# Last weights' decoding every 7 products in two expert tiles, and attention's row weighings ranked among its operations

## The chip, the cores and the metric

The kernel runs on one core of one Trainium2 chip. The metric is the device time of one execution in microseconds; the median of several runs counts. In what follows TensorE (PE) multiplies matrices, VectorE (DVE), ScalarE (ACT) and GpSimd (POOL) work on elements, and SyncE (SP) issues most of the transfers.

## What is computed

Three stages follow one another, all in float32:

```python
# 1. attention: 2 batches x 8 heads, 576 positions, 64 per head, rotary embedding
attn = softmax(rotate(q) @ rotate(k).T / 8);  x = (attn @ v)      # 1152 tokens x 512
# 2. experts: each token goes to one of 8 experts
logits = x @ w_gate + modality_bias[modality_id];  e = argmax(logits);  p = softmax(logits)[e]
y = p * (relu(x @ w1[e]) @ w2[e])                                 # 512 -> 1024 -> 512
# 3. last feed-forward
h = y @ w_in;  g = h * tanh(log1p(exp(h)));  out = g @ w_out      # 512 -> 2048 -> 512
```

## The kernel before

**Precision.** Every float32 product is done as three products of a high and a low half: high x high, high x low, low x high. ScalarE makes a high half by a copy, VectorE or GpSimd the low half by a subtraction. So one product group of an expert tile's first layer has 4 x 3 = 12 TensorE products, one of the second layer 8 x 3 = 24.

**Attention and its plan.** The operations of attention are given to a planner (class Plan) with an engine, a cost, a rank (the smaller, the earlier) and what they depend on. The planner simulates the engines' queues and so fixes each engine's order: when an engine is free, it takes the ready operation of lowest rank among the first 40 of its list, or else the one that can start earliest. Ranks near the end of attention lie between 140 and 176: the last maxima of the scores at about 151 and 154, the low halves of the transposed probabilities up to 158, the normalisations at 155.5, 156.1, 166.2 and 175.7. Into this plan the start of the experts is woven: once half of the tokens are routed, the first expert tile's 304 rows are loaded (xrow), weighed by their gate value on VectorE (x_gate, L1301, three row tiles of 128, 128 and 48 rows), transposed on TensorE (x_tr, L1312, into banks of the scores) and split into halves (x_hi, x_lo). These operations have rank 900, behind all of attention. Beside them GpSimd starts on the low halves of the expert weights (L611).

**Expert tiles.** Four tiles of 304 rows follow, two for each half of the tokens; here they are called tiles 1 to 4. A tile has 8 groups of 12 products (hidden layer, L705; after each a relu on ScalarE, L728, and the low half of it on VectorE, L730), then 4 groups of 24 products (output, L705), and four transposed row groups of the next tile (L669, L676) after the second of them. Expert weights come in chunks of 512 KB. PSUM has seven buffers for the products.

**Decoding of the last weights.** The weights of stage 3 come as 16 chunks of 1 MB of 64-bit numbers, through two buffers (wr, L1382), and VectorE makes float32 chunks (wc) of them with three operations: L1398, L1403, L1408. During the expert tiles each operation handles half a chunk (512 columns) and goes through a PSUM tile (rt); a chunk is then six counts. In the last stage an operation handles 1024 columns and counts two. The next load into a buffer is issued by SyncE two counts after the chunk in it is done. While tiles are computed, `drive` takes up a count whenever a running counter of TensorE steps is a multiple of `every`:

```python
if y[0] != "pe":
    continue
nq_[0] += 1
if nq_[0] % every == 0:
    decode(1, limit)
```

The value of `every` is `P['dec'][0]`, 12, for tiles 1 and 2 (no decoding in the last two groups of tile 2), `P['dec'][1]` for tile 3 and `P['dec'][2]` for tile 4, where the limit is 72 counts, twelve chunks. Before tile 1's products reach `drive`, the routing of the second half of the tokens has drawn some of them ahead.

**Last stage.** It runs over two groups of tokens (640 and 512) and, in each, over 16 chunks of the hidden width. For each chunk TensorE makes h (L1578, 12 products for each half of the tokens, three PSUM buffers), ScalarE three steps towards tanh (L1593 to L1597), VectorE a reciprocal (L1604) and a multiplication that also frees the buffer of h (L1605), ScalarE and GpSimd the halves of g (L1616, L1622), and TensorE adds the chunk's share to the output (o, L1639). Its order is written out by times in units of half a chunk. Decoding is put into it in two ways, in the first group of tokens:

```python
if 3 <= q < FC2:
    at2(m + 0.6, decode, 2)
if q < FC2:
    for z in range(3):
        at2(m - 4.05 + 0.6 * z, lambda n=6 * q + 2 * z + 2: decode(n - nd[0]))
```

Of the kernel before, what the change touches and what calls it, by code (L numbers as in the profile page):

```python
# [35 lines left out]
FC2 = F2 // 128  # L36

Q = {'r0': 2.45, 'rd': 2.0, 'tanh': 1.06, 'rec': 1.1, 'hi': 2.2, 'lo': 2.38, 'o': 3.86}
P = {'sd': (4,), 'dl': (28, 44), 'qd': (2, 3), 'alt': (0.1, 4), 'd0': 82, 'vl': 24, 'w3': 3, 'rq': (0.2, 2.3, 0.55, 0.25), 'dec': (12, 9, 8), 'rl': 3, 'ah': 0, 'eps': 0.05, 'slack': 0.1}
K = {'ld': -22.67, 'prep': (-24.92, -22.38, -23.33, -27.14, -20.49, -7.62), 'sc': (-8.42, -3.18, 1.68, 1.67, 2.84, 10.44, 1.99, 8.05, 9.75), 'max': (-2.26, -5.46, -1.21, -1.85, 5.06, 8.41, 4.71, 11.42, 13.72), 'exp': (-3.19, 1.66, 6.32, 3.7, 13.26, 11.14, 14.6, -2.87, 25.74), 'tr': (0.69, 2.1, 2.56, 2.68, 5.53, 7.5, 8.45, 9.85, 10.88, 11.85, 15.56, 16.66, 16.92, 19.98), 'hi': (-3.91, -0.31, 2.51, 3.62, 4.25, 4.9, 5.01, 5.32, 7.26, 9.77, 13.56, 14.12, 14.6, 15.66), 'lo': (0.77, 1.83, 5.61, 6.34, 6.67, 7.32, 10.02, 10.73, 12.18, 13.92, 13.94, 14.62, 17.33, 18.02), 'pv': (7.08, 7.84, 10.5, 10.69, 14.13, 14.25, 14.32, 15.96, 18.04, 20.31, 21.03, 22.86, 23.97, 25.61), 'evac': (14.53, 9.65, 6.27, 25.13), 'rec': (-4.7, -0.45, 4.11, 12.71), 'fmm': (4.53, -3.79, 16.24, 17.22), 'norm': (15.5, 16.11, 26.18, 35.69)}  # L40

QT = [(0, 128), (128, 128), (256, 64), (320, 128), (448, 128)]
# [31 lines left out]
class Plan:  # L74
# [39 lines left out]
    def pick(self, e):  # L114
        best, lines = None, set()
        for o in self.todo[e][:40]:
# [8 lines left out]
            if best is None or t < best[0] - 1e-9:  # L125
                best = (t, o)
            if t <= self.free[e] + P["eps"]:
                break
# [40 lines left out]
    def run(self):  # L169
# [3 lines left out]
        while any(self.todo.values()):  # L173
            best = None
            for e in self.todo:
                c = self.pick(e)
                c = c and (c[0], 1, c[1])
                for o in self.alt[e][:4]:
# [4 lines left out]
                    t = max(t, self.free[e])  # L183
                    if (c is None or t + o[4] - P["alt"][0] <= c[0]) and t + o[4] + P["alt"][1] < end:
                        c = (t, 1, o)
                for st in self.streams:
# [3 lines left out]
                    if st["gate"] and not st["gate"](t):  # L190
                        continue
                    if c is None or t + (st["next"][1] - P["slack"] if e in st["low"] else 0.0) <= c[0]:
                        c = (t, 0, st)
# [19 lines left out]
def moe_kernel(ctx: ExitStack, tc: tile.TileContext, aps, out):  # L213
# [17 lines left out]
    def heads(x):  # L231

        return x[..., 0:XC].rearrange("p j (h e) -> p j h e", h=H)
# [325 lines left out]
    xrow, wraw, whl = {}, {}, {}  # L559
# [15 lines left out]
    def load_rows(k):  # L575
        r = regs[k]
        pool = mp if k != "x" else wpool[-1]
        xrow[k] = t = pool.tile([128, 3, RW], F32, tag="xrow", name=f"xrow{k}")
        for i, (r0, rn) in enumerate(TCH):
            ld = nc.sync.dma_start(out=t[:rn, i], in_=scratch[ds(r["c"] + r0, rn), :])  # L580
            if k != "x":
                after_scatters(ld, k[0])
# [18 lines left out]
    def split_chunk(k, i):  # L601
# [5 lines left out]
        lo = pool.tile([128, 1024], F32R, tag="wlo", name=f"wlo{k}_{i}", bufs=n)  # L607
        dve = k == (0, 0) and i in P["sd"]
        yield ("dve", 1.14, False) if dve else ("pool", 2.3, False)
# [71 lines left out]
    def moe_tile(k, feed, bank):  # L681
# [28 lines left out]
        for f in range(FC1):  # L710
# [7 lines left out]
            )  # L718
            if f == P["rl"] and nxt in regs and nxt not in feed.rows:
                feed.rows.add(nxt)  # L720
# [13 lines left out]
        for d in range(KC):  # L734
            i = 4 + d
            ends = k == (0, 1)
            if ends and d >= P["qd"][0]:
                yield "quiet"
# [79 lines left out]


    def attention(actx, hook):  # L820
        a_c = actx.enter_context(tc.tile_pool(name="a_const", bufs=1))
        p2 = actx.enter_context(tc.tile_pool(name="a_p2", bufs=2))
# [404 lines left out]
        op("ids", "act", 0.1, 30.0, setup_ids)  # L1227
        op("bias", "pool", 2.5, 60.0, setup_bias, deps=[("ids",)])
        hook(plan, bank, ltile)
        plan.run()  # L1230

# [12 lines left out]
    def route(b):  # L1244
        yield from routing(b, lambda: cur["rbank"]())

    def tile_rows(b):
        for i in range(2):
            regs[b, i] = tile_regs(tbl[b][:, i])

    def until_pe(gen):
        for y in gen:
            if y[0] in ("pe", "mark"):
                return
            yield y

    def hook(plan, bank, ltile):

        r0 = route(0)
        cur["rbank"] = lambda: bank("counts")  # L1260

        def until_mark():
            for y in r0:
                if y[0] == "mark":
                    return
                yield y

        def mark(name):
            return lambda t: plan.done.update({name: ("dve", t)})

        def start():
            plan.add(until_pe(r0), plan.now, end=mark("rt"), gate=cur["spare"])

        def rest():
            next(r0)
            plan.add(until_mark(), plan.now + 1.0, end=mark("rt_row"))

        def scatter():
            plan.add(cur["scatters"], plan.now, low=("pool",), end=mark("rt_sc"))

        def table():
            plan.add(r0, plan.now, end=mark("rt_end"))

        def weights():
            tile_rows(0)
            load_rows(K0)
            feed.rows.add(K0)
            plan.done["xrow"] = ("sp", plan.now + 7.8)
            plan.add(until_pe(gen0), plan.now + 3.9, low=LOW)

        K0, n0, xg = (0, 0), B * H - 1, []

        def x_gate(i):
            x, rn = xrow[K0], TCH[i][1]
            if not xg:
                gated.add(K0)
                t = mp.tile([128, FC1, T], F32R, tag="hl", name=f"xg{K0}").bitcast(F32)
                xg.append(t.rearrange("p a t -> p (a t)")[:, 0:3 * DM].rearrange(
                    "p (i d) -> p i d", i=3
                ))  # L1300
            nc.vector.tensor_scalar(  # L1301
                out=xg[0][:rn, i].rearrange("p (h e) -> p h e", h=H),
                in0=heads(x)[:rn, i, :, 0:D], scalar1=x[:rn, i, XC + 1:XC + 2], scalar2=None,
                op0=ALU.mult,
            )

        def x_bank(c):
            return ltile[3 + c // 2][:, c % 2]

        def x_tr(c, i):  # L1310
            r0, rn = TCH[i]
            nc.tensor.transpose(  # L1312
                out=x_bank(c)[:, r0:r0 + rn], in_=xg[0][:rn, i, c * 128:(c + 1) * 128],
                identity=ident[:rn, :rn],
            )

        def x_hi(c):
            if K0 not in xsplit:
                xsplit[K0] = tuple(
                    mp.tile([128, KC, T], F32R, tag=t, name=f"{t}{K0}") for t in ("xh", "xl")  # L1320
                )
            nc.scalar.activation(out=xsplit[K0][0][:, c], in_=x_bank(c)[:, :T], func=AF.Copy)

        def x_lo(c):
            xh, xl = xsplit[K0]
            nc.vector.tensor_tensor(
                out=xl[:, c], in0=x_bank(c)[:, :T], in1=xh[:, c].bitcast(F32), op=ALU.subtract
            )

        def x_op(name, eng, dur, fn, *a, deps):  # L1330
            plan.op((name,) + a, eng, dur, 900.0, lambda: fn(*a), deps=deps)

        for i in range(3):
            x_op("gate", "dve", 0.6, x_gate, i, deps=["xrow"])
        for c in range(KC):
            for i in range(3):
                x_op("xtr", "pe", 0.11, x_tr, c, i,
                     deps=[("gate", i), ("exp", n0, 1, c // 2, 3 + c // 2)])
            x_op("xhi", "act", 0.31, x_hi, c, deps=[("xtr", c, i) for i in range(3)])
            x_op("xlo", "dve", 0.39, x_lo, c, deps=[("xhi", c)])  # L1340

        z = 10.0 * H
        plan.op(
            "route", "sp", 0.0, z, start,
            deps=[("norm", n, f) for n in range(H) for f in range(2)],
        )
        plan.op("rt_mm", "pe", 0.43, z, lambda: next(r0), deps=["rt"], take=[("ring", "rt")])
        plan.op("rt_cp", "dve", 1.1, z, rest, deps=["rt_mm"], give=[("ring", "rt")])
        plan.op("scatter", "sp", 0.0, z, scatter, deps=["rt_row"])
        plan.op("table", "sp", 0.0, z, table, deps=["rt_row", ("plo", B * H - 1)])  # L1350
        plan.op(
            "rows", "sp", 2.2, z, weights,
            deps=["rt_end", "rt_sc", ("stack", B * H - 1), ("vload", B * H - 1)],
        )
# [14 lines left out]
    with ExitStack() as actx:  # L1369
        attention(actx, hook)  # L1370
# [414 lines left out]
```

## Time and profile before

| what | value |
|---|---|
| median of 3 runs | 493.33 us (492.34 to 494.33) |
| the profiled execution | 493.86 us, span 492.1 us |
| TensorE busy | 470.1 us, 96% of the span |
| VectorE busy | 392.3 us, 80% |
| GpSimd busy | 361.2 us, 73% |
| ScalarE busy | 332.6 us, 68% |
| reciprocals on VectorE (L1604) | 64, 124.6 us |

The span goes from the first to the last instruction; the execution's time also holds what lies around it. Times in rows are microseconds from the span's start unless marked as nanoseconds. In a timeline a row is: start, duration, engine, line, operation, what it writes and reads, how often in a row, and in brackets the idle time of its engine before it and what ended it. Attention takes up about the first third, the expert tiles run until about 281 us, and the last stage from there.

### The profile page before, as it was taken

The page shows a single profiled execution, that of the slowest core. Times are in us where ns is not written, and L with a number is a line of the kernel's source. Part 1 is how long each engine was busy: PE and PEld are TensorE (multiplying, and loading weights), DVE is VectorE, ACT ScalarE, POOL GpSimd, SP SyncE. Part 2 cuts the span into 40 slices and gives each one's busy share as a digit, 9 for nine tenths or more (in the row PEclk, how much of TensorE's full clock was granted, in tenths as well). Part 3 has the DMA queues.
Part 4 walks back from the last instruction along what each step waited for, and adds up shares of the span by engine and source line. Part 5 has one row for each costly group of instructions (what it writes and reads, how often), then busy time and mean ns, then how long its engine had stood idle before and what let it go on. Part 6 is the DMA issues. An engine that isn't in the chain of part 4 may idle for free.

```text
span 492.1 us, 8772 instructions
## 1 busy us (share of the span) xinstructions
PE 470.1 (96%) x2996; PEld 430.1 (87%) x2996; DVE 392.3 (80%) x613; ACT 332.6 (68%) x753; POOL 361.2 (73%) x363
## 2 busy tenths in 40 slices
PE   2899999999999999999999999999998999999995
PEld 1799999999989899999999998998986887888894
DVE  6599898899889774644677799999999859777773
ACT  4598888768868565565654586766745778777763
POOL 3799999999962686768667377778765759987654
PEclk9999999999999999999999999999999899999999
DMA  6779986868664796969864310202020001100002
GB/s 221 176 201 233 228 231 152 215 173 198 154 171 144 265 392 250 348 256 305 304 220 172 116 56 1 86 2 86 1 85 1 1 1 43 43 23 1 1 0 87
DMA packets 24131, 69.41 MB, mean 141 GB/s; under 512 B 5522, under 2 KB 9810, under 8 KB 22034
## 3 DMA queue, kind: packets, MB, share of 16 engines
q1 hardware_dynamic: 21794, 63.16, 41.8%
q0 software_dynamic: 1456, 5.03, 2.6%
q10 hardware_dynamic: 832, 0.61, 0.5%
q8 instruction: 25, 0.41, 0.3%
q14 instruction: 24, 0.20, 0.1%
HBM read 49.08 MB, written 6.44 MB: 113 GB/s over the span
## 4 chain that ended last, share of the span: by engine, by line
PE 38%; DVE 11%; issue 3%; ACT 1%; POOL 0%; POOLq 0%; DVEq 0%; ACTq 0%
PE h L1578 14%; PE o L1639 13%; PE mm L705 11%; DVE ta L1604 8%; DVE ta L1605 1%; DVE wc L1403 1%; DVE wc L1398 1%; DVE wc L1408 0%; PE mm L669 0%; POOL out_dram L1649 0%; POOLq L1781 0%; DVE idi L1725 0%; ACT ot L1645 0%; DVE yl L1516 0%; ACT ta L1597 0%
## 5 line engine op out<-in xcount | busy, mean ns | idle before, releaser
L1604 DVE RECIPROCAL ta<-ta 128x320 f32<-128x320 f32 (+1 forms) x64 | 124.6, 1947 | 22.5 <-ACT ta L1597 22.5
L1552 POOL TENSOR_TENSOR w2l<-wc,w2h 128x512 fp32r<-128x512 f32 x64 | 88.8, 1409 | 16.4 <-ACT w2h L1551 8.3
L1639 PE MATMUL o<-w2h,g 128*128 128x512 f32 x288 | 98.3, 397 | 0.1
L1622 POOL TENSOR_TENSOR g<-ta,g 128x320 fp32r<-128x320 f32 (+1 forms) x63 | 52.8, 842 | 32.9 <-ACT g L1616 21.3
L972 PE MATMUL sc<-sk,sq 128*128 128x288 f32 (+1 forms) x320 | 59.4, 315 | 11.5 <-ACT sk L901 7.6
L1578 PE MATMUL h<-yh,w2h 128*128 128x320 f32 (+2 forms) x204 | 67.5, 331 | 2.2 <-DVE ta L1605 2.2
L1578 PE MATMUL h<-yl,w2h 128*128 128x320 f32 (+2 forms) x204 | 67.3, 330 | 0.1
L1578 PE MATMUL h<-yh,w2l 128*128 128x320 f32 (+2 forms) x204 | 67.3, 330 | 0.0
L1639 PEld LDWEIGHTS o<-w2h,g 128*128 128x128 f32 x288 | 54.4, 189 | 12.2 <-POOL g L1622 0.7
L1040 ACT ACTIVATE ph<-pt 128x512 fp32r<-128x512 f32 (+2 forms) x112 | 54.6, 509 | 13.5 <-PE pt L1020 12.7
L1007 ACT ACTIVATE pexp<-sc,nm 128x576 f32<-128x576 f32 x72 | 53.3, 740 | 15.4 <-DVE nm L996 11.6
L996 DVE TENSOR_REDUCE nm<-sc 128x1 f32<-128x576 f32 x72 | 53.7, 753 | 11.1 <-PE sc L972 6.9
L972 PEld LDWEIGHTS sc<-sk,sq 128*128 128x128 f32 (+1 forms) x320 | 46.5, 190 | 14.4 <-ACT sk L901 8.0
L1639 PE MATMUL o<-w2l,g 128*128 128x512 f32 x144 | 57.0, 396 | 0.0
L1020 PE MATMUL pt<-ident,pexp 128*128 128x128 f32 (+1 forms) x360 | 55.1, 278 | 0.7 <-DVE tbl L521 0.6
L1061 PE MATMUL av<-ph,vhl 128*128 128x256 f32 (+1 forms) x160 | 51.0, 335 | 0.1
L1046 DVE TENSOR_TENSOR pl<-pt,ph 128x512 fp32r<-128x512 f32 (+1 forms) x80 | 48.8, 628 | 1.9 <-ACT ph L1040 1.5
L1593 ACT ACTIVATE ta<-h 128x320 f32<-128x320 f32 (+1 forms) x64 | 25.6, 400 | 29.3 <-PE h L1578 29.3
L1020 PEld LDWEIGHTS pt<-ident,pexp 128*128 128x128 f32 (+1 forms) x360 | 42.1, 137 | 3.6 <-PE pt L1020 0.8
L1578 PEld LDWEIGHTS h<-yh,w2h 128*128 128x128 f32 x204 | 38.5, 189 | 7.1 <-DVE ta L1605 3.3
L1616 ACT ACTIVATE g<-ta 128x320 fp32r<-128x320 f32 (+1 forms) x64 | 27.9, 436 | 22.6 <-DVE ta L1605 22.4
L1578 PEld LDWEIGHTS h<-yl,w2h 128*128 128x128 f32 x204 | 38.6, 189 | 4.0 <-DVE yl L1516 0.4
(448 smaller groups left out, 1211.8 us busy)
## 6 DMA issues: line engine op xcount, KB each, us to landing
wr<-in_wio_dram SPq DMA_DIRECT2D x16, 1024.0 KB, 6.1
wc<-in_w_dram SPq DMA_DIRECT2D x26, 512.0 KB, 5.0
xs<-in_qk_dram SPq DMA_DIRECT2D x15, 576.0 KB, 5.2
sk<-ab SPq DMA_DIRECT2D x30, 288.0 KB, 3.8
sq<-ab SPq DMA_DIRECT2D x30, 144.0 KB, 2.4
vraw<-in_v_dram SPq DMA_DIRECT2D x16, 160.0 KB, 4.1
scratch<-zero SPq DMA_DIRECT2D x12, 108.8 KB, 4.5
xrow(0, 0)_2295<-scratch SPq DMA_DIRECT2D x2, 290.0 KB, 3.0
```

Of the source, the lines that this page charges most:

```text
L705: nc.tensor.matmul(ps[:, :T], lhsT=w, rhs=m, start=(n == 0), stop=(n == 3 * len(pairs) - 1))
L972: nc.tensor.matmul(t[:m, hf, :NC2], lhsT=sq[:, c:c + m], rhs=sk[:, z, hf * NC2:(hf + 1) * NC2], start=(z == 0), stop=(z == 1),)
L996: nc.vector.tensor_reduce(out=nm[n, j], in_=sc[n, j][:, :, :NC2], axis=AX.XY, op=ALU.max, negate=True)
L1007: nc.scalar.activation(out=pe, in_=sc.pop((n, j))[:, :, :NC2], func=AF.Exp, bias=nm.pop((n, j)), accum_out=st[n, hf][:, i:i + 1],)
L1020: nc.tensor.transpose(out=t[:kn, o:o + 128], in_=pexp[n, j][:, k0:k0 + kn], identity=ident)
L1040: nc.scalar.activation(out=block(ph, n, hf, kts, slice(0, kn)), in_=psum(n, hf, kts, kn), func=AF.Copy)
L1061: nc.tensor.matmul(av[n, hf][:, :u.nq], lhsT=vhl[n][:, kt].rearrange("p a d -> p (a d)"), rhs=src[:, kt, u.at:u.at + u.nq], start=(kt == 0 ...
L1552: nc.gpsimd.tensor_tensor(out=lo[:, cs], in0=w[:, cs], in1=hi[:, cs].bitcast(F32), op=ALU.subtract)
L1578: nc.tensor.matmul(ps[:, :w], lhsT=wt[:, c], rhs=m[y][:, c], start=(n == 0), stop=(n == 11))
L1604: nc.vector.reciprocal(out=ta, in_=ta)
L1622: eng.tensor_tensor(out=gt[q][1][:, o:o + w], in0=tas.pop((q, i))[:, :w], in1=gt[q][0][:, o:o + w].bitcast(F32), op=ALU.subtract,)
L1639: nc.tensor.matmul(acc[g, t], lhsT=a[:, s], rhs=b, start=(f == 0 and z == 0), stop=(f == FC2 - 1 and z == 2),)
```

## The change

The step of decoding in tiles 3 and 4 goes from 9 and 8 products to 7 and 7. The three row weighings get ranks of their own, 162, 165 and 150, instead of 900, and a cost of 0.5 instead of 0.6 us in the plan. What the operations compute stays the same.

```diff
-P = {..., 'dec': (12, 9, 8), ...}
+P = {..., 'dec': (12, 7, 7), ...}
...
         for i in range(3):
-            x_op("gate", "dve", 0.6, x_gate, i, deps=["xrow"])
+            plan.op(
+                ("gate", i), "dve", 0.5, (162.0, 165.0, 150.0)[i], lambda i=i: x_gate(i),
+                deps=["xrow"],
+            )
```

## Rows read from the trace of the kernel before

**Rows 1.** The chain of waits, in order of time: start, duration, what

```profile
223.82 20.29 PE mm L705 x144
...
310.08 2.16 DVE ta L1604
...
379.68 2.86 PE h L1578 x12
...
386.40 2.10 PE o L1639 x9
388.49 1.76 PE h L1578 x12
```

**Rows 2.** TensorE's waits, 140 to 281 us: total, times, longest

```profile
PE sc L1312 <- DVE xg(0, 0)_2437 L1301: 1.1, 1, 1.1
```

**Rows 3.** TensorE's timeline, 369 to 385 us

```profile
369.33 0.40 PE L1639 MATMUL o<-w2h,g 128*128 128x512 f32 x1
370.16 0.41 PE L1578 MATMUL h<-yh,w2h 128*128 128x320 f32 x1 [0.43 <-DVE ta L1605]
...
379.68 0.42 PE L1578 MATMUL h<-yh,w2h 128*128 128x320 f32 x1 [1.78 <-DVE ta L1605]
...
384.48 0.31 PE L1578 MATMUL h<-yh,w2h 128*128 128x320 f32 x1
```

**Rows 4.** Windows: PE, PEld, DVE, ACT, POOL busy, TensorE's clock, DMA share, GB/s

```profile
369.00:385.00 16.00, 13.68 (x65) 11.23 (x64) 15.41 (x13) 9.74 (x22) 9.62 (x9) 0.89 0.01 2
385.00:393.00 8.00, 8.00 (x44) 7.07 (x43) 6.56 (x6) 5.08 (x12) 4.65 (x5) 1.00 0.00 0
```

**Rows 5.** Windows, operations on wr alone: VectorE busy (count), clock, DMA share, GB/s

```profile
0.00:217.80 217.80, 13.75 (x20) 1.00 0.76 225
217.80:251.40 33.60, 15.13 (x22) 1.00 0.76 266
251.40:281.00 29.60, 16.51 (x24) 1.00 0.43 158
281.00:400.00 119.00, 25.61 (x15) 0.99 0.11 36
```

**Rows 6.** VectorE's timeline, 370 to 377 us

```profile
370.02 0.69 DVE L1398 TENSOR_SCALAR wc<-wr 128x1024 int32<-128x1024 int32 x1
370.63 2.15 DVE L1604 RECIPROCAL ta<-ta 128x320 f32<-128x320 f32 x1
...
373.21 2.01 DVE L1403 SCALAR_TENSOR_TENSOR wc<-wr,wc 128x1024 int32<-128x1024 int32 x1
...
376.96 2.14 DVE L1604 RECIPROCAL ta<-ta 128x320 f32<-128x320 f32 x1
```

**Rows 7.** The tile wr: nanoseconds min/median/max, starts, shapes; its loads' landing

```profile
L1398 DVE TENSOR_SCALAR rt<-wr x22: 682/685/696, 182.6 to 278.3; 128x512 int32<-128x512 int32 x22
...
L1398 DVE TENSOR_SCALAR wc<-wr x5: 687/770/1776, 299.1 to 370.0; 128x1024 int32<-128x1024 int32 x5
...
DMA to landing us min/median/max: 4.9/6.1/12.0
```

**Rows 8.** VectorE's timeline in tile 3

```profile
228.29 0.69 DVE L1403 SCALAR_TENSOR_TENSOR rt<-wr,rt 128x512 int32<-128x512 int32 x1
229.01 0.69 DVE L1408 SCALAR_TENSOR_TENSOR wc<-wr,rt 128x512 int32<-128x512 int32 x1
...
237.92 0.47 DVE L730 SCALAR_TENSOR_TENSOR hl(1, 0)_3538<-mm,hh(1, 0)_3537 128x304 fp32r<-128x304 f32 x1 [0.61 <-ACT hh(1, 0)_3537 L728]
238.31 0.68 DVE L1398 TENSOR_SCALAR rt<-wr 128x512 int32<-128x512 int32 x1
```

**Rows 9.** VectorE's timeline at the end of attention

```profile
158.21 0.48 DVE L1301 TENSOR_SCALAR xg(0, 0)_2437<-xrow(0, 0)_2295 128x512 f32<-128x512 f32 x1
...
158.90 2.31 DVE L1301 TENSOR_SCALAR xg(0, 0)_2437<-xrow(0, 0)_2295 48x512 f32<-48x512 f32 x1
```

**Rows 10.** GpSimd's timeline there

```profile
158.43 2.49 POOL L611 TENSOR_TENSOR wlo(0, 0)_0_2459<-wraw(0, 0)_0_2358,whi(0, 0)_0_2371 128x1024 fp32r<-128x1024 f32 x1 [2.09 <-ACT whi(0, 0)_0_2371 L606]
```

## What is predicted

> **What bounds the kernel now.** I read the chain of waits first, in order of time. Through the expert tiles it is nothing but TensorE's products, 0.141 us each (20.29 / 144); at 310 us it passes to VectorE's reciprocals, and at 379.68 back to TensorE, where it stays to the last stores [rows 1]. So there are two regimes: where TensorE runs without a gap, only fewer TensorE gaps can help, and between 310 and 380 VectorE may be the bound.
>
> TensorE's gaps settle how much that is worth. From attention's end to the end of the expert tiles there is one long gap: 1.1 us before a transpose of the weighed rows, waiting for a row weighing on VectorE [rows 2]. In the last stage TensorE is back to back until 369.33, although VectorE is already on the chain: it was late, but within the slack of the three PSUM buffers of h. Then it waits 0.43 us at 370.16 and 1.78 us at 379.68, both for the VectorE operation that frees such a buffer [rows 3]. The windows show what follows: the granted clock is 0.89 in 369 to 385 and 1.00 after, so behind the idle time some products ran at 1.2 instead of 2.4 GHz [rows 4].
>
> I price that whole stretch at once. From 369.33 to 384.48 TensorE issued 36 products of h and 22 of o. At full clock twelve h take 1.76 us and nine o 2.10 us [rows 1]: 36 x 0.147 + 22 x 0.233 = 10.4 us. It took 15.15 us [rows 3]; 4.7 us are lost to VectorE being late, the slow clock included.
>
> **Edit 1, the decoding.** A chunk of last weights is six counts of decoding (2 halves x 3 operations) while it goes through PSUM, and three operations twice as wide in the last stage. Operations on the loaded words: 20 before tile 3, 22 in its order, 24 in tile 4's, and 15 in the last stage [rows 5]: 66 counts, eleven chunks, then five chunks of three. The counter of products stands at 290 when tile 3 begins (392 products and transposes of the first two tiles, less the 102 that the routing of the second half drew ahead; 290 / 12 gives 24, but the quiet end of tile 2 starts at 242, which gives the 20 seen). Tile 3 has 196 steps and tile 4 has 192: every 9 gives 22, every 8 gives 24, as seen. Every 7: 69 - 41 = 28 and 96 - 69 = 27, capped by the limit of 72. So 72 counts are reached at step 165 of tile 4, twelve chunks are ready before the last stage, and four are left in it: six more operations in the tiles, three fewer later.
>
> *What is saved.* The last stage decodes two counts per f chunk from the fourth on, and on demand if that lags. Started at 66 it lags: near the end two chunks' operations fall between five reciprocals (one, two, one, two). Started at 72, nothing comes on demand until the last chunk: one operation, then two together, then none. Up to the one before them all stays as it was. The chunk no longer decoded there costs VectorE 0.61 us (370.02 to 370.63) and 3.75 us (373.21 to 376.96), 4.4 us in all [rows 6]. By the release that TensorE waited for at 379.68 VectorE is then 4.4 us earlier, at about 375.3; TensorE without its earlier losses comes to that point at 376.6 (369.33, then 24 products of h and 16 of o). At 370.16 VectorE is 3.7 us earlier, since two of a chunk's three operations are gone by then. So both waits go with 1.3 us to spare, and with them the slow clock behind them. If the remaining first operation takes its longest 1.78 us instead of 0.69 [rows 7], the spare is 0.2 us, still no wait. Value taken: the whole 4.7 us. Lower bound: the spare is missed by a little, the idle time shrinks by less than 2.2 us and the slow clock stays: 2 us. After 384 the chain is TensorE's own, so the gain reaches the end.
>
> *What it costs in the tiles.* Six operations of 0.69 us [rows 7] on VectorE, 4 us, beside TensorE. In a first product group (96 products, 13.5 us) VectorE then has 13.7 x 0.72 + 8 x 0.39 = 13.0 us of work, start to start [rows 8]: full, not over. What is queued behind a decode is the low half of h; TensorE wants the eighth low half 22 products (3.1 us) after the group's end, near 240.3 in tile 3 (223.8 + 117 x 0.141). Before, it began at 237.92. Laying the new order out by these durations I get about 238.5, 0.6 us later and 1.3 us in time. After the cap VectorE has only Y's splitting to do, so the start of the last stage, which hangs on ScalarE and one such split, is not touched.
>
> *The loads.* A buffer is freed by a chunk's sixth count and wanted again six counts later. In tile 3 the fourth chunk's last operation comes at 228.3 to 229.0 (before at 229.01), and the sixth chunk, which takes its buffer, is wanted near 235.0: six us against a landing time of 4.9 / 6.1 / 12.0 us [rows 7]. I take 6.1: a wait of 0.1 to 0.2 us, in a slack of 1.3. SyncE's queue holds expert chunks behind these loads; they wait for a VectorE operation that now ends earlier, and are split long before they are used. Cost taken: nothing; upper bound in the rival below.
>
> **Edit 2, the weighings.** Three operations per row tile keep their work and move in VectorE's order. The second and third began at 158.21 and 158.90, and the third, the smallest (48 rows), took 2.31 us where the one of 128 rows took 0.48 [rows 9]. It began while GpSimd's low half of the first expert chunk ran, 158.43 to 160.92, and ended 0.2 us after it [rows 10]; the planner counts 0.6 us for it. That is TensorE's 1.1 us gap. With due time 150 the third goes first as soon as the rows are in, ahead of the last maxima and low halves (rank 151 to 158), well before GpSimd's 158.43, and should take no more than 0.48 us there. The other two (162, 165) stay behind the low halves, about where the first two weighings were. Two more low halves that stood behind the long weighing come earlier with it. Value taken: the gap of 1.1 us goes. Bounds: 0 (below) and 1.1; a loss of up to 1 us if a weighing now first in the queue waits for its rows, or holds up a maximum.
>
> VectorE's second SBUF port is shared with GpSimd, and two-port operations and GpSimd's block each other, says the Trainium skill (Advanced Engine Details and Errata, VectorE Performance Modes, the note under the mode summary). The 2.31 us agree. By that rule the order matters only if no weighing falls into GpSimd's stretch at all; if one does, edit 2 is worth nothing, and the sum is 488.6.
>
> **The sum.** The profiled execution took 493.86 us (span 492.1 and 1.8 around it): 493.86 - 4.7 - 1.1 = 488.1. It lies 0.5 above the median of the runs, 493.33, so I forecast 487.5 us for the median.
>
> **Rivals.**
> - *The second weighing takes the third's place.* One operation of up to 0.48 us is put ahead, so the 128-row weighing of 158.21 may start at 158.69, inside GpSimd's 158.43 to 160.92, and last until about 161.1 as the third did. For it: 0.22 us of distance before, less than the shift. Against: idle gaps in VectorE's order ahead of it that swallow the shift. Time: 493.3 - 4.7 = 488.6. Chance 0.22.
> - *The last stage gives back only part.* TensorE's next limit comes at once, or the clock still falls; or a weighing waits for its rows: 489.5 to 491. For it: the spare is only 0.2 to 1.3 us. Chance 0.13.
> - *The edit does not do what it says:* the count stops short of 72 and five chunks remain, so only edit 2 counts: 492.3. Against it: the same arithmetic gives 20, 22 and 24 before. Chance 0.06.
> - *Slower: loads arrive late in the tiles.* A decode waiting for its load holds the low halves behind it. From a landing time of about 7.5 us on, TensorE waits in tile 3; at the 12.0 us that occurred once, the sixth chunk's first operation moves from 235.0 to 241.0, the last two low halves come near 243, and TensorE stands about 3 us and then pays some 2.5 us for the restart and the slow clock, as around 380 (4.7 less the idle 2.2). Twice, in tiles 3 and 4: 11 us, less 5.8: 498.5. For it: DMA share 0.76 in tile 3 [rows 5]. Against: the median of 6.1. Chance 0.09.
>
> **Chances.** Forecast, both gaps gone: 0.50. What a measurement can tell from no change is about 0.5%, 2.5 us, so the forecast, the first rival and most of the second are faster: 0.81; same 0.10; slower 0.09. The range runs from 486.4 (forecast less the runs' scatter of 1 us) to 490.9, which takes in the first rival and most of the second, and leaves out the last two.
>
> **What would show it.** Right: 12 wide decode operations in the last stage instead of 15; 28 and 24 in the tiles; no TensorE wait for VectorE between 369 and 380 and a clock of 1.00 there; the weighings all near 0.5 us, and no 1.1 us gap before the transposes. Wrong: TensorE waits inside tiles 3 and 4, VectorE idle time ended by the loads there, a weighing of 2.3 us, or a fall of the clock at another place of the last stage.

## The result, and the profile after

The changed kernel takes 488.68 us (median of 6 runs, 488.45 to 489.36) beside 494.56 us of the kernel before (492.34 to 495.1): a ratio of 0.9891, interval 0.987 to 0.9912. Forecast was 487.5 us, range 486.4 to 490.9. The profiled execution took 488.63 us, its span is 486.9 us.

The last stage first. Its chain of waits, which passed to VectorE at 310 us before [rows 1], is now TensorE's products alone:

```profile
309.36 1.76 PE h L1581 x12
311.12 2.10 PE o L1642 x9
...
376.28 1.75 PE h L1581 x12
378.03 1.39 PE o L1642 x6
379.42 1.77 PE h L1581 x12
```

Up to 385 us twelve h take 1.75 to 1.77 us each time, and nothing stands between them and the o. TensorE's products at the two places where it waited before [rows 3] start without a wait:

```profile
369.11 0.30 PE L1581 MATMUL h<-yh,w2h 128*128 128x320 f32 x1
376.12 0.30 PE L1581 MATMUL h<-yh,w2h 128*128 128x320 f32 x1
```

The windows of the stretch in which TensorE was busy for 13.68 of 16 us at a clock of 0.89 [rows 4] (columns as there):

```profile
369.00:385.00 16.00, 16.00 (x93) 14.62 (x92) 15.44 (x11) 9.46 (x21) 12.37 (x10) 1.00 0.01 2
```

The windows of the operations on wr alone, as [rows 5]:

```profile
0.00:217.80 217.80, 14.17 (x21) 1.00 0.76 226
217.80:251.40 33.60, 18.55 (x28) 1.00 0.74 273
251.40:281.00 29.60, 16.83 (x25) 1.00 0.58 212
281.00:400.00 119.00, 21.04 (x12) 1.00 0.06 19
```

28 operations in tile 3, 25 in tile 4, and 12 of 21.04 us instead of 15 of 25.61 us in the last stage.

The weighings on VectorE's timeline, which took 0.48 and 2.31 us [rows 9]:

```profile
154.44 0.47 DVE L1301 TENSOR_SCALAR xg(0, 0)_2423<-xrow(0, 0)_2295 48x512 f32<-48x512 f32 x1
155.65 0.47 DVE L1301 TENSOR_SCALAR xg(0, 0)_2423<-xrow(0, 0)_2295 128x512 f32<-128x512 f32 x1
157.29 0.46 DVE L1301 TENSOR_SCALAR xg(0, 0)_2423<-xrow(0, 0)_2295 128x512 f32<-128x512 f32 x1
```

All three are short. But TensorE's waits from 140 to 281 us (total, times, longest) show that the 1.1 us of [rows 2] have a successor:

```profile
PE mm L705 <- POOL wlo(0, 0)_5_2744 L611: 1.2, 1, 1.2
PE pt L1020 <- DVE tbl L521: 0.6, 1, 0.6
PE xo L1091 <- ACT avt L1070: 0.5, 1, 0.5
```

The first line is new: a product of tile 1 waits for the low half of the sixth expert chunk, wlo_5 (chunks are numbered from 0), on GpSimd. The third is new as well; behind that product of attention (xo) TensorE is 0.94 us ahead of the kernel before, where it was 0.46 us ahead earlier, so this wait costs nothing.

**Where the time came from.** I compare the same TensorE operations in both timelines. At 146 us, before any order differs, the changed kernel is 0.46 us ahead (145.69 against 146.15). Its first expert product starts at 162.89 instead of 164.66, 1.77 us ahead. Behind the wait for wlo_5 and through the last stage up to 367 us it is 0.46 us ahead again. Between 367 and 384.5 us that grows to 5.22 us and stays. So, in this pair of profiles, 4.76 us come from the last stage, nothing from the weighings in the end, and 0.46 from a start that no edit touched: 5.22 of the 5.23 us between the two profiled executions.

### The profile page after: what moved, and what is told of

Its sections match the earlier page's. It is cut to its first block, busy times and chain, and to the rows that moved or that the text cites. A ratio compares the mean times of both kernels' runs of the same rounds, so it can differ in the third digit from the quotient of the medians.

```text
span 486.9 us, 8783 instructions
## 1 busy us (share of the span) xinstructions
PE 466.0 (96%) x2996; PEld 428.0 (88%) x2996; DVE 389.1 (80%) x616; ACT 332.5 (68%) x753; POOL 361.8 (74%) x363
## 4 chain that ended last, share of the span: by engine, by line
PE 52%; POOL 0%; issue 0%; ACT 0%; POOLq 0%; DVE 0%
PE h L1581 21%; PE o L1642 20%; PE mm L705 11%; PE mm L669 0%; POOL out_dram L1652 0%; POOLq L1784 0%; ACT ot L1648 0%; DVE yl L1519 0%; ACT yh L1517 0%; ACT Y L755 0%; POOL spacer L1659 0%; POOLq L1652 0%
## 5 line engine op out<-in xcount | busy, mean ns | idle before, releaser
L1555 POOL TENSOR_TENSOR w2l<-wc,w2h 128x512 fp32r<-128x512 f32 x64 | 90.3, 1432 | 16.4 <-ACT w2h L1554 8.3
L1625 POOL TENSOR_TENSOR g<-ta,g 128x320 fp32r<-128x320 f32 (+1 forms) x63 | 51.7, 826 | 27.7 <-ACT g L1619 21.0
L1596 ACT ACTIVATE ta<-h 128x320 f32<-128x320 f32 (+1 forms) x64 | 25.6, 401 | 30.7 <-PE h L1581 28.8
L1581 PEld LDWEIGHTS h<-yh,w2l 128*128 128x128 f32 x204 | 38.4, 188 | 2.3
```

The source lines that it names most:

```text
L1555: nc.gpsimd.tensor_tensor(out=lo[:, cs], in0=w[:, cs], in1=hi[:, cs].bitcast(F32), op=ALU.subtract)
L1581: nc.tensor.matmul(ps[:, :w], lhsT=wt[:, c], rhs=m[y][:, c], start=(n == 0), stop=(n == 11))
L1625: eng.tensor_tensor(out=gt[q][1][:, o:o + w], in0=tas.pop((q, i))[:, :w], in1=gt[q][0][:, o:o + w].bitcast(F32), op=ALU.subtract,)
```

## Experiments

The median of the kernel before beside these runs was 493.2 us for e1 to e4, 493.34 for e5 to e8 and 494.87 for e9 to e11; each time below is to be read against its own.

### 1. Edit 1 alone (e1_decoding_alone)

```diff
-'dec': (12, 9, 8)
+'dec': (12, 7, 7)
```
on the kernel before.

> Edit 1 alone: steps of 7 and 7, the weighings as before. Theory (the last stage's VectorE lateness is the whole of edit 1's gain): 4.7 us under the kernel before, no TensorE wait for VectorE between 369 and 385, clock 1.00 there; the 1.1 us gap before the transposes and the weighing of 2.3 us are still there. Rival (part of the 5.2 us comes from an interplay of both edits): clearly less than 4.7, 3 to 4 us.

Measured: 488.85 us (488.6 to 489.85), ratio 0.9909 (0.9888 to 0.993). The third weighing still takes 2.31 us and TensorE waits its 1.1 us for it. Yet the products of the last stage start 0.04 us before those of the full change. In these two profiles edit 1 alone gives the whole gain.

### 2. Edit 2 alone (e2_ranks_alone)

The changed kernel with `'dec': (12, 9, 8)`, as before.

> Edit 2 alone: the ranks, with steps of 9 and 8. Theory (given back): TensorE starts the first expert tile some 1.3 us earlier, and waits about 1.2 us for the low half of chunk 5 on GpSimd near 181; the time is 0 to 0.5 us under the kernel before. Rival (the prediction's term): 1.1 us under it, with no such wait.

Measured: 492.13 us (491.76 to 493.84), ratio 0.9988 (0.9972 to 1.0004): the interval takes in no difference, and the median, 1.07 us below that of the kernel before, cannot decide between the theory and its rival. The profile can: TensorE waits 0.9 us for wlo_5, as the theory says, and 0.4 us of a lead of 1.3 us at the first expert product are left behind that wait.

The profile shows something else. TensorE's timeline in the last stage has the same two waits, to 0.01 us, as [rows 3]:

```profile
369.89 0.41 PE L1581 MATMUL h<-yh,w2h 128*128 128x320 f32 x1 [0.43 <-DVE ta L1608]
379.39 0.41 PE L1581 MATMUL h<-yh,w2h 128*128 128x320 f32 x1 [1.78 <-DVE ta L1608]
```

but the clock behind them did not fall. Windows around the second wait, of this kernel and then of the kernel before:

```profile
376.00:384.00 8.00, 6.22 (x35) 5.32 (x35) 7.53 (x6) 4.50 (x11) 4.03 (x4) 1.00 0.00 1
```

```profile
376.00:384.00 8.00, 6.21 (x23) 5.24 (x24) 7.54 (x6) 4.22 (x10) 3.74 (x4) 0.79 0.00 1
```

The busy times agree; in them 35 products ran at 1.00, which is 2.4 GHz, and 23 at 0.79, a mean of 2.4 and 1.2 GHz. Here the stretch costs 3.20 us against the changed kernel (products from 0.18 to 3.38 us late), in the kernel before 4.76. So of edit 1's 4.7 us some 3.2 are the waits and some 1.6 the slow clock, which this execution was spared. (The 3.2 are counted from start to start; the brackets, 2.21 us together, count only from the end of the product ahead.)

The runs of this kernel fall into two groups, 491.76 to 492.18 and 493.12 to 493.84, about that far apart, and the mean granted clock of each run parts them in the same way: 0.997 to 1.000 in the seven of the first group, 0.994 or 0.995 in the five of the second. For the kernel before, beside e5 to e8, it is the same: eight runs of 491.85 to 493.37 us at 0.997 to 1.000, five of 494.47 to 495.16 at 0.994 or 0.995. None of the changed kernel's twelve runs is under 0.997. The profiles agree: both with a mean of 0.994, the kernel before and the run of experiment 4, have the fall behind a second wait of 1.78 us (0.70 at 381 to 384 us in the latter), and the one here, at 0.998, has none.

### 3. Doses of decoding (e4_count69, e7_count60, e5_count78)

```diff
-'dec': (12, 7, 7)
+'dec': (12, 9, 7)      # e4_count69
+'dec': (12, 9, 11)     # e7_count60
+'dec': (12, 7, 6)      # e5_count78, with drive(last, P["dec"][2], 78)
```
on the changed kernel.

> Both edits' ranks, steps of 9 and 7: 69 counts before the last stage, half a chunk less than 72. Theory (a threshold: VectorE has 1.3 us to spare with 72, and has here one narrow operation of 0.6 us more by the second wait): no TensorE wait for VectorE, the time of the changed kernel within 0.4 us. Rival (gain in proportion to the counts): half of the gain, 2.4 us over the changed kernel.

> The dose the other way: the changed kernel with 9 and 11 products for a count instead of 7 and 7, so that about 60 counts are reached and some 18 wide operations stay in the last stage (12 in the changed kernel, 15 in the kernel before). Theory (beyond about 13 operations VectorE is the bound in the last stage, and each further one costs TensorE its own duration, some 1.4 us): three more operations than the kernel before are 4.4 us more than the 3.1 to 4.8 lost there: 496 to 498, TensorE waits for ta or g in several units from about 320 us on, and the clock falls in some of them. Rival (only the last units matter, because the work is done on demand near the end): 2 us or less above the kernel before, 494 to 495.5.

> The changed kernel with one more count step in the same direction: in tile 4 every 6 products instead of 7, and the limit at 78 instead of 72, so that thirteen chunks are ready and nine wide operations stay in the last stage instead of twelve. Theory (the gain ended where TensorE stopped waiting for VectorE; in the changed kernel TensorE has no gap there, so less work on VectorE is worth nothing): the time of the changed kernel, 488.4 +- 0.5, VectorE's decoding time in the last stage about 4 us lower, TensorE's unit starts there unchanged. Rival 1 (the time goes with the number of operations left, whatever TensorE does): 1 to 4 us below the changed kernel, 484 to 487. Rival 2 (tile 4 is full: 28 counts there plus the six more push a low half past its time): a TensorE wait on hl in tile 4, 489 to 492.

Measured: 491.89 us (491.25 to 493.04), ratio 0.9975 (0.9961 to 0.9989), for 69 counts; 496.04 us (495.06 to 497.83), 1.0054 (1.0034 to 1.0074), for 60; 489.75 us (489.42 to 490.86), 0.9925 (0.9901 to 0.995), for 78. The windows of the operations on wr in the last stage, of 69, 60 and 78 counts:

```profile
281.00:400.00 119.00, 25.47 (x15) 1.00 0.08 28
```

```profile
281.00:400.00 119.00, 30.08 (x18) 0.99 0.12 43
```

```profile
281.00:400.00 119.00, 18.06 (x10) 1.00 0.06 19
```

(The tenth of the last is a narrow one that began at 280.6.) Between 302 and 386 us TensorE's products fall behind those of the changed kernel (21.04 us of decoding, no wait) by 7.7 us with 30.08 us of decoding, by 2.8 with 25.47, and by 3.2 to 4.8 with the 25.6 of the order before.

My theory for 69 counts fell. I took the number of counts for what matters, and three fewer to be harmless. But half a chunk begun in the tiles is finished in the last stage in narrow operations, and on VectorE's timeline there

```profile
298.84 0.50 DVE L1401 TENSOR_SCALAR wc<-wr 128x512 int32<-128x512 int32 x1
299.38 1.67 DVE L1406 SCALAR_TENSOR_TENSOR wc<-wr,wc 128x512 int32<-128x512 int32 x1
306.14 1.78 DVE L1411 SCALAR_TENSOR_TENSOR wc<-wr,wc 128x512 int32<-128x512 int32 x1
```

two of the three last as long as wide ones, which go to 1.78 us and above, while in the tiles the same shape, by way of PSUM, takes 0.69. So VectorE had 25.47 us of decoding, as much as in the kernel before with 25.61, and the time went back with it. Half a chunk less was worth nothing here.

With 60 counts the theory holds: VectorE is the bound, and a further chunk, 4.5 us more on VectorE, costs TensorE 4.5 us more than the 3.2 of experiment 2. In both the clock behind the last of these waits is 1.00.

With 78 counts the rival that the time goes with the number of operations left falls: with 9 wide operations left, TensorE's products go no faster than in the changed kernel (0.69 us behind it from 295 to 360 us, then 1.08). Up to 281 us this kernel was 1.19 us ahead of the changed kernel, since TensorE did not wait for wlo_5 in it (experiment 6). What it lost lies at the start of the stage. TensorE's waits from 281 us on:

```profile
PE h L1581 <- DVE yl L1519: 2.1, 1, 2.1
```

and VectorE's timeline at the end of tile 4:

```profile
277.33 0.69 DVE L1401 TENSOR_SCALAR rt<-wr 128x512 int32<-128x512 int32 x1
277.93 2.01 DVE L1519 TENSOR_TENSOR yl<-Y,yh 128x320 fp32r<-128x320 f32 x2
...
280.59 0.69 DVE L1411 SCALAR_TENSOR_TENSOR wc<-wr,rt 128x512 int32<-128x512 int32 x1
281.19 2.00 DVE L1519 TENSOR_TENSOR yl<-Y,yh 128x320 fp32r<-128x320 f32 x2
```

Decoding now goes on up to the last split of Y, which TensorE's first product of the stage wants. In the changed kernel that split starts at 280.34 and takes 0.93 us. This is rival 2 of the expectation, at another place than I named; the time that my theory gave, 488.4 +- 0.5 us, was missed by it.

### 4. Why the weighing took 2.31 us (e6_before_chunk0_vector)

```diff
-'sd': (4,)
+'sd': (0, 4)
```
on the kernel before: the low half of the first expert chunk moves to VectorE.

> One look at the kernel before with one edit: the low half of the first expert chunk is computed by VectorE instead of GpSimd, so that GpSimd does nothing while the row weighings run. Theory (the third weighing took 2.31 us because GpSimd's low half ran beside it): the third weighing takes 0.45 to 0.5 us, though it still stands where it stood in the order, and TensorE's 1.1 us wait before the transposes of the weighed rows is gone or under 0.3. Rival (the 48-row weighing is slow by itself, or its rows come late): it stays at 2.0 to 2.4 us. Time within 1.5 us of the kernel before either way.

Measured, one run: 495.48 us at a mean granted clock of 0.994. That is 2.1 above the median of the kernel before, where I had given 1.5 at most, but 0.3 to 1.0 above its runs at 0.994 or 0.995. VectorE's timeline:

```profile
158.24 0.47 DVE L1301 TENSOR_SCALAR xg(0, 0)_2437<-xrow(0, 0)_2295 48x512 f32<-48x512 f32 x1
...
161.65 3.37 DVE L611 TENSOR_TENSOR wlo(0, 0)_0_2459<-wraw(0, 0)_0_2358,whi(0, 0)_0_2371 128x1024 fp32r<-128x1024 f32 x1
```

At the same place in the order, with GpSimd idle, the weighing takes 0.47 us: GpSimd beside it was the cause, and the 1.1 us wait before the transposes is gone. The second row shows the price from the other side: VectorE's own low half now fell beside GpSimd's next one (161.58 for 2.35 us) and took 3.37 us, where later such a one takes 1.2. TensorE waits 1.7 us for it.

### 5. What became of edit 2's gain (e3_chunk5_on_vector, e8_no_ranks_chunk5_vector)

One edit, made to the changed kernel (e3) and, with `'dec': (12, 7, 7)`, to the kernel before, so without edit 2 (e8):

```diff
-'sd': (4,)
+'sd': (4, 5)
```

> Both edits, and the low half of the first tile's chunk 5 on VectorE as that of chunk 4 already is, so that it no longer stands behind the five indirect transfers in GpSimd's queue. Theory (the gain of edit 2 is lost in GpSimd's queue): the wait of 1.2 us near 181 goes, 1.0 to 1.4 us under the changed kernel. Rival (the chunks themselves come too late, the DMA queues being full): TensorE waits there as long or for chunk 6, and the time is that of the changed kernel.

> The kernel before with edit 1 (the decoding) and the fifth chunk's low half on VectorE, without edit 2 (the weighings as before). Theory (edit 2 gains about 1.3 us at the start of tile 1 and loses it where TensorE waits for the fifth chunk's low half in GpSimd's queue; with that low half on VectorE some of it is kept): without edit 2 nothing is waiting to be given back, so this kernel is near edit 1 alone, 488.6 to 489.2, and 0.5 to 1.0 above the changed kernel with the fifth low half on VectorE (488.04). Rival (moving the fifth low half is worth the 0.6 by itself, edit 2 is worth nothing even then): 488.0 to 488.2.

Measured: 488.04 us (487.87 to 488.05), ratio 0.9886 (0.9864 to 0.9909), with edit 2; 489.76 us (489.55 to 490.0), 0.992 (0.9899 to 0.994), without it. Both lie above what I expected, the first 0.6 us below the changed kernel instead of 1.0 to 1.4, the second 0.6 above the top of its range. The wait for wlo_5 is gone in both, and now edit 2 is worth something: the first expert product starts at 163.11 instead of 164.44, and that lead, 1.33 us, is still 1.37 at 302 us. In the pair without this edit (the changed kernel and experiment 1) a lead of 1.27 us at the first product had become 0.04 the other way. So the gain is real, and in that pair it was the wait for wlo_5 that took it back. Some 0.5 to 0.7 us are lost in both for a new reason: VectorE's wlo_5 stands ahead of low halves of the hidden layer, and TensorE's products come late at 180.2 and 180.7 us (in the first). Of the 1.7 us between the two medians 0.4 arise near 361 us, where one product of o follows the one ahead after 0.5 instead of 0.23 us, with no wait named; e5, e6 and e9 to e11 show the same. Their times tell what it waits for: it starts 0.06 us after the end of GpSimd's low half of g (361.52 after 361.47 in the run without edit 2, 361.44 after 361.38 with 78 counts, 360.84 after 360.78 in e11). So that chain is close behind TensorE in the last stage, and the second run lost 0.4 us to it, which edit 2 has no part in.

### 6. The chain behind wlo_5 (e9_chunk1_vector, e10_chunk3_vector) and the changed kernel again (e11_changed_again)

GpSimd's timeline of the changed kernel:

```profile
162.16 2.39 POOL L611 TENSOR_TENSOR wlo(0, 0)_1_2519<-wraw(0, 0)_1_2369,whi(0, 0)_1_2471 128x1024 fp32r<-128x1024 f32 x1 [1.53 <-ACT whi(0, 0)_1_2471 L606]
...
169.68 2.42 POOL L611 TENSOR_TENSOR wlo(0, 0)_3_2626<-wraw(0, 0)_3_2573,whi(0, 0)_3_2624 128x1024 fp32r<-128x1024 f32 x1 [2.20 <-ACT whi(0, 0)_3_2624 L606]
172.24 1.96 POOL L409 DMA_INDIRECT scratch<-X,row  x1
...
178.29 0.97 POOL L409 DMA_INDIRECT scratch<-X,row  x1 [0.23 <-issue]
...
179.32 2.39 POOL L611 TENSOR_TENSOR wlo(0, 0)_5_2744<-wc,whi(0, 0)_5_2742 128x1024 fp32r<-128x1024 f32 x1
```

GpSimd's order is fixed: wlo_5 stands behind five scatters of routed rows, these behind wlo_3. TensorE's first expert product comes 1.77 us earlier than before; wlo_5 begins only 0.23 us earlier, at 179.32 instead of 179.55. The first scatter takes 1.96 us, the others less than 1. VectorE's timeline beside it, with the low half of the fifth chunk (wlo_4):

```profile
172.05 1.23 DVE L611 TENSOR_TENSOR wlo(0, 0)_4_2694<-wc,whi(0, 0)_4_2692 128x1024 fp32r<-128x1024 f32 x1 [0.47 <-ACT whi(0, 0)_4_2692 L606]
```

and GpSimd's and VectorE's timelines of the run with 60 counts, whose tile 1 has the same order:

```profile
171.83 1.05 POOL L409 DMA_INDIRECT scratch<-X,row  x1 [0.17 <-issue]
...
177.99 2.42 POOL L611 TENSOR_TENSOR wlo(0, 0)_5_2744<-wc,whi(0, 0)_5_2742 128x1024 fp32r<-128x1024 f32 x1
```

```profile
171.94 1.23 DVE L611 TENSOR_TENSOR wlo(0, 0)_4_2694<-wc,whi(0, 0)_4_2692 128x1024 fp32r<-128x1024 f32 x1 [0.47 <-ACT whi(0, 0)_4_2692 L606]
```

There the scatter began 0.11 us ahead of wlo_4 and took 1.05 us, TensorE does not wait for wlo_5, and its lead reaches the last stage whole; the run with 78 counts is the same. In all thirteen profiles the twelve scatters that began 0.11 us or more behind the start of such a low half of VectorE, while it ran, ended 0.80 to 0.93 us after that one's end; the five that overlap one but began ahead of it, or within 0.04 us of its start, took 1.05. So in this kernel it hangs on a few tenths of a microsecond whether edit 2 pays.

Two edits move one of the low halves ahead of it to VectorE, on the changed kernel:

```diff
-'sd': (4,)
+'sd': (1, 4)      # e9_chunk1_vector
+'sd': (3, 4)      # e10_chunk3_vector
```

> The changed kernel with the low half of the second expert chunk on VectorE too (it stands there after the split of the first rows, where VectorE was idle for 0.67 us). Theory (TensorE's 1.2 us wait for the sixth chunk's low half, wlo_5, comes from a chain: the second chunk's low half on GpSimd ends late, frees the buffer of the fourth chunk's load late, and so holds GpSimd's low half of that one, the scatters behind it and the sixth chunk's low half behind those): with the second low half done about 1 us earlier, the sixth begins near 178.3 instead of 179.32 and TensorE's wait shrinks from 1.2 to 0.2 to 0.4, without a low half of VectorE ahead of TensorE's needs later: 487.5 to 488.0, 0.6 to 1.0 below the changed kernel. Rival (the scatters wait for the routing's own results, not for the fourth chunk's low half): the sixth chunk's low half begins at 179 or later, wait 1.0 to 1.6, time as the changed kernel or 0.5 above, since VectorE's added operation holds up the routing.

> The changed kernel with the fourth chunk's low half on VectorE too. It stands directly ahead of the scatters on GpSimd (169.68 to 172.10), so GpSimd is free of it. By the chain of the run above (GpSimd's queue decides): scatters begin as soon as the weighing column is there, near 171 to 172, the sixth low half at 177.5 to 179, TensorE's wait 0 to 1.0. Rival (on VectorE it delays the routing operations and low halves of h that stand behind it by 1.2 us): scatters begin no earlier than 172, small TensorE gaps on hl between 170 and 176; time as the changed kernel +- 0.4.

> The changed kernel once more, on the same chip as the two runs above, so that differences under 1 us can be read: 488.0 to 489.0, TensorE's only waits between 160 and 281 the same as in its first profile (1.2 for the sixth low half), none between 281 and 480, granted clock 1.00 in 369 to 385.

Measured: 487.52 us (487.3 to 487.82), ratio 0.9859 (0.984 to 0.9877), with the second low half moved; 489.69 us (489.26 to 490.16), 0.9904 (0.9888 to 0.9921), with the fourth; 489.17 us (488.88 to 489.75), 0.9893 (0.9877 to 0.991), for the changed kernel itself, whose wait for wlo_5 is 0.9 us in this profile. GpSimd's timeline with the second low half moved:

```profile
168.84 2.40 POOL L611 TENSOR_TENSOR wlo(0, 0)_3_2626<-wraw(0, 0)_3_2573,whi(0, 0)_3_2624 128x1024 fp32r<-128x1024 f32 x1 [1.12 <-ACT whi(0, 0)_3_2624 L606]
171.40 1.05 POOL L409 DMA_INDIRECT scratch<-X,row  x1 [0.16 <-issue]
...
177.89 2.40 POOL L611 TENSOR_TENSOR wlo(0, 0)_5_2744<-wc,whi(0, 0)_5_2742 128x1024 fp32r<-128x1024 f32 x1
```

The fourth begins 0.84 us earlier, the scatters too, and so the first of them begins ahead of VectorE's wlo_4 (171.97) and takes 1.05 instead of 1.96 us (the second, caught by the end of wlo_4, 1.30); wlo_5 begins 1.43 us earlier and nobody waits for it. TensorE enters the last stage 1.2 us ahead of the changed kernel. With the fourth moved, GpSimd is free and yet the scatters begin later: its timeline says for whom they wait,

```profile
173.12 1.05 POOL L409 DMA_INDIRECT scratch<-X,row  x1 [5.61 <-DVE rt L431]
```

for routing operations of VectorE, ahead of which the added low half had waited 1.76 us for its high half and then run 1.23 us. TensorE waits 0.7 us for a hidden group instead. So both chains are real: without the fourth low half ahead of them the scatters wait for VectorE's routing. The second low half has room on VectorE, the fourth does not. The changed kernel itself is here 0.17 us above the range that I gave, and the version with the fourth moved 0.52 above it, where I gave 0.4 at most. The version with the second moved is the fastest seen, 1.65 us below the changed kernel beside it, and all five of its runs lie below all six of that one.

## Why the forecast was nearly right

**The bound.** Right. In the last stage VectorE was the bound and the decoding its surplus; experiment 3 moves the time up with it, and below the 12 operations of the changed kernel, with 9, nothing more is gained.

**Edit 1, the saving (4.7 us).** Right as a sum: 4.76 measured. The counts came out as worked out (28 in tile 3, 24 in tile 4, where the window counts 25 since operations on an edge stand in two windows, and 12 wide operations left), no wait is left between 369 and 380 us, and the clock is 1.00. The release that TensorE had waited for at 379.68 now comes at 374.73, 1.4 us before the product at 376.12; I had 1.3 to spare. What I had not seen is that the term has two parts of different standing: 3.2 us of waits, which the profiles of before and of experiment 2 both have, and 1.6 us of slow clock, which the first has and the second has not. A term read from one profile holds for executions like that one.

**Edit 1, the cost in the tiles (nothing).** Right. In tile 3 VectorE's eighth low half began at 237.53, which is 0.07 us later than in [rows 8] once the 0.46 us lead is taken off; I had 0.6. The loads landed in 4.7 / 5.3 / 14.4 us. One came late enough to hold VectorE for 6.0 us, at 179.9 to 185.9 in tile 1, another for 0.61 us until 252.31; no TensorE wait follows from either. That the work after the cap "has only Y's splitting to do" carried more than I gave it: with 78 counts that split is late and costs 2.1 us.

**Edit 2 (1.1 us).** The step that failed. Its mechanism came as forecast: the third weighing goes first, all three take 0.47 us, and the long one was long because GpSimd ran beside it, which experiment 4 shows. The rule of the Trainium skill quoted in the prediction (Advanced Engine Details and Errata, VectorE Performance Modes) agrees with the first row there, 0.47 us with GpSimd idle; the second, 3.37 us, is a subtraction of two tensors, and the rule as quoted speaks of two-port operations only. (The prediction's "three operations per row tile" is a slip: there is one for each of the three row tiles.) The gap of 1.1 us did go, and the first expert product gained 1.31 us beyond the lead. What failed is the step from a gap closed at the start of tile 1 to the end of the kernel: I did not ask which of TensorE's next operands comes from a queue that does not move with it. GpSimd's queue did not, and wlo_5, which had ended 0.4 us before its use while TensorE was late (179.55 + 2.40 against 182.34), became the next limit some 18 us on. Value of the term in the profiled execution: 0 instead of 1.1, its lower bound. In the other profiles with the same tile 1 it is 0.2 to 0.4 us where a scatter was held up beside VectorE's wlo_4 (experiment 2, 69 counts, e11) and 1.4 to 1.5 us, kept up to the last stage, where none was (60 and 78 counts): the size of the term is not fixed by the order alone.

**The sum.** 493.86 - 4.76 - 0 - 0.46 is 488.64, measured 488.63; forecast 488.1 for this execution. The 0.46 is luck: without the early start, which no edit made, the forecast for this execution would have been 1.0 us too low, nearly the whole of edit 2's term. For the median, forecast from three runs of the kernel before, it is 1.2 too low. The first rival, with 488.6, has the time but not the cause: no weighing fell beside GpSimd. The rival of late loads did not come about, nor did the count that stops short.

## What to carry to other kernels

When a gap of the bounding engine closes, its later operands are wanted earlier: follow the next stage's operands on every queue (here GpSimd's, behind scatters that wait for other things) before the gap is counted as gain, and look for the low-priority work in that queue that another idle engine can take. Size a queue's surplus in busy time of the engine in that stage: half a chunk saved returned nothing here, since two of its three operations took as long there as whole ones. A low half moved to another engine can also hold up the queue that it left: look at which of the two begins first. And where a stall is followed by a slow clock, price the two apart, since the second need not come in each execution.

## What was not expected of the hardware

- The granted clock after the same idle time differs between executions: behind a wait of 1.78 us it was 0.79 (376 to 384 us, kernel before) and 1.00 (experiment 2). What decides it is not shown. Within one profile, that of 60 counts, a wait of 1.84 us ending at 361.57 us was followed by 0.78 and 0.82 (360 to 363 and 363 to 369 us), and one of 1.77 us ending at 382.46 by 1.00 (376 to 384 and 385 to 393).
- Operations of VectorE that run beside GpSimd's low halves can take two to three times as long: a subtraction on 128 x 1024 elements took 1.2 us in tile 1 and 3.37 us beside GpSimd's, the first decoding operation on 128 x 1024 in the last stage 0.69 with GpSimd idle (370.02, kernel before) and 1.76 to 1.78 within a low half of GpSimd's, the split of Y (two of 128 x 320) 0.89 and 2.01 us. GpSimd's own low half of 128 x 1024 took 2.35 to 2.51 us either way.
- GpSimd's indirect scatters pay in the other direction: 0.92 to 1.05 us in tile 1, but 1.75 to 1.97 when they began just behind the start of VectorE's subtraction on 128 x 1024.
